# A four-layer kernel (two S4 convolutions, two sliding attentions): the written orders of all five plans laid anew

## The chip, the cores and the metric

The kernel runs on one core of one Trainium2 chip. The core has engines with instruction streams of their own: TensorE (PE, with its weight loads as PEld), VectorE (DVE), ScalarE (ACT), GpSimd (POOL) and SyncE (SP), whose queue issues most DMAs (SPq). Each engine takes its instructions strictly in the order in which they were written; an instruction that waits for another engine holds up everything behind it on its own.

The metric is the time of one execution on the device, in microseconds (us), as the median over runs. A profiled execution has a time of its own beside the span that its trace covers.

## The reference, cut to what matters

The input is one sequence `x` of 2048 positions by 512 channels, in bf16. Four layers follow, each with a residual and a layer norm ahead: S4, attention, S4, attention.

```
def _A_ref(u, ...):            # S4: a kernel K of 2048 taps per channel, then a causal convolution by FFT
    A = A_re + 1j*A_im; dB = exp(log_dt) * (B_re + 1j*B_im); Cc = C_re + 1j*C_im
    P = exp(dt*A * l)          # l = 0..2047, 128 modes per channel
    K = einsum("dn,dnl,dn->dl", Cc, P, dB).real
    y = irfft(rfft(pad(u)) * rfft(pad(K)))[:L] + u * Dskip
def _B_ref(x, wqkv, wo):       # 32 heads of 16; each position sees itself and 7 others, 2 apart
    logits = einsum(q, k at pos - 2*w) * scale, -1e9 where pos - 2*w < 0
    o = einsum(softmax(logits), v at pos - 2*w);  return o @ wo
x = x + _A_ref(layernorm(x)); x = x + _B_ref(layernorm(x))
x = x + _A_ref(layernorm(x)); x = x + _B_ref(layernorm(x))
```

The same parameters serve both S4 layers, so the taps K are built once.

## The kernel before

The sequence lies in SBUF as `X` (128 partitions, 16 columns `j` of 512 channels each) and stays there through all four layers. The program is five plans, run one after another, with no barrier between them:

- Plan 0, `prepare` (L501): the parameters, a ladder of powers of the modes by repeated squaring (`sq`, `lad`, `l`: the square on ACT at L623, the rest on DVE at L631 and L635), multiplier tables from it (`MUA`, `MUB`, `MPA`, `MPB`, one half each at L595 on ACT or L607 on DVE), the first tables of powers `Ttab` (L407 to L428), and the first layer norm, whose sums come from PE as `gram` and `rows` (L678, L682). The first products of the raw parameters (`t`, `quad`, L512) wait for their loads.
- Plan 1, `kernel_and_first_conv` (L724): for eight half-blocks of channels the tables of powers (DVE L412 to L428 and L476, with sums on PE L451 and evictions on ACT L456), the contraction with C and B on PE (L489), the spectra of taps and input (first Fourier step on PE, L863, evicted to `Z` on ACT, L868; transposes by DMA, L877, or on PE; a second step), the product `pa` on DVE (L953), the inverse (`vp`, `VT`) and the output `ps_y` (L997, L1000), evicted to `X` at L1004. The spectrum of the taps goes to DRAM as `kt_scratch`.
- Plan 2, `b_layer` (L1313): transposes of X or U to U (by DMA L1368, or PE L1362 with an ACT copy L1365), q and k (`ps_qk` L1483, evicted to `qT` and `kT` at L1488), a shifted copy of kT (by DMA or by ACT, L1499), products q times k on DVE (`prod` L1556, 2.2 us each), sums of them on PE (`Lp` L1567), softmax pieces (`L`, `LT`, `sm`, a mask by POOL at L1643, the scaling of the logits at L1636), v (`ps_v` L1511, evicted to `VX` at L1522), products with v on DVE (`prod` L1732), sums on PE (`po` L1748, L1753), evictions `ot` on ACT (L1766), transposes of them by DMA (`oT<-ot`, L1771), and the output projection (`ps_o` L1832) added into X. The adding has several ways: a DVE add straight from PSUM (L1804), an ACT eviction (L1810) with a DVE add (L1813) or with an accumulating DMA issued by POOL (L1816), or an identity matmul on PE (L1829) that adds X in PSUM, with an ACT eviction (L1934 to L1936). Then the layer norm for the next plan (`U`, on ACT L1946 or DVE L196).
- Plan 3, `a_layer` (L1160): the convolution again with the taps' spectrum loaded as `Kt` (sixteen loads on SP, L1298): first Fourier step `ps_s` (L1183) evicted to `Z` (L1187), transposes `zt<-Z` by DMA (L1198) or PE, second step `xp` (L1222 to L1225) evicted to `xc` (L1229), products `pa` (L1239 to L1245), inverse `vp` (L1259, L1263) evicted to `VT` (L1266), outputs `ps_y` (L1285) evicted to X (L1290).
- Plan 4: `b_layer` again, with the output stores on SP (L1970) in place of a layer norm.

No scheduler sets an order while the kernel is built. Each plan first records all its operations with a number each, and `Plan.run` then emits them in the order of a list of numbers written out by hand, one string for each plan (`ORDERS`, L215). Where an operation can be done in several ways (`either`, `moved`, `halved`), each way has numbers of its own, and the way whose numbers stand in the list is the one taken. So the lists set both the order on every engine and the engine of each operation that has a choice. Buffers are reused from small pools (in plans 1 and 3 four PSUM slots `psA`), and a write waits until the slot's last reader is done. The loads of parameters and of the input are issued before plan 0 and are in no list.

Some operations by number, as the prediction's steps and the diff need them:

- Plan 0: 25, 24, 19 are the raw products C_im by B_re, C_re by B_im and C_re by B_re; 26 adds the first two; 14 is the first `quad`; 271, 272, 261 table multiplies; 216 the use of `gram` (L684).
- Plan 1: 330 a first Fourier step on PE, 299 and 300 the sum L452 and its eviction, 301 the table multiply L427 behind it; 429 the product of block 1, part 0, 370 its input's eviction; 237 a store to `k_scratch`; 774 the last `ps_y`, 776 and 775 its eviction on DVE and on ACT.
- Plan 2: 507, 513, 511 products with v; 522 the scaling of the logits L1636.
- Plan 3: 342 and 343 the last eviction of `Z` on ACT and on DVE; 88 the first product; 283 the eviction of `VT` of block 2, part 1, whole on DVE; 408, 411 outputs.
- Plan 4: 417, 500, 497 the transposes L1771; 796, 816, 759 output projections; 508 a sum `po`; 799 an output projection with the identity matmul; 442, 487, 489 products.

Line numbers in the text are those of the profile (where a helper records an operation, the line is the one that emits the instruction).

Of the kernel before, what the change touches and what calls it, by code (L numbers as in the profile page):

```python
# [198 lines left out]
def load_params(nc, pp, prm):  # L199
# [16 lines left out]
    "1 187 185 2 3 7 8 5 9 10 11 12 19 25 24 189 195 14 26 13 256 20 30 27 31 21 34 23 35 45 42 49 38 55 47 48 201 43 "  # L216
    "57 56 39 203 59 61 67 197 199 60 258 69 76 75 68 259 71 260 72 263 83 81 73 87 264 215 84 93 267 95 213 268 88 "
    "85 193 96 191 105 207 100 118 106 205 116 119 120 124 99 209 211 107 128 132 111 134 130 271 135 131 110 280 216 "
    "281 142 218 261 140 146 283 143 219 144 147 108 262 217 284 265 154 266 220 158 152 156 285 125 272 221 155 278 "
    "168 170 222 286 171 159 164 166 269 247 287 229 239 231 233 270 167 273 237 179 178 243 176 288 274 289 275 236 "  # L220
    "276 225 97 223 251 253 227 245 249 241 277 255 279",
    "1 69 70 71 67 68 72 33 2 39 42 40 80 81 82 43 83 0 36 34 37 9 45 86 87 88 77 84 46 49 79 30 89 90 54 199 200 78 "
    "202 203 204 205 47 92 48 206 59 52 53 18 10 19 119 165 20 120 121 122 133 11 134 139 208 209 123 125 126 127 128 "
    "129 210 93 94 136 137 96 97 142 140 143 211 98 27 131 216 28 99 222 57 155 156 62 100 166 159 63 157 144 218 223 "
    "58 158 220 150 219 102 221 224 151 167 162 103 173 163 169 310 311 312 104 105 174 171 313 168 170 152 316 29 "
    "110 317 318 172 64 175 319 153 314 320 284 285 287 288 289 181 117 147 178 182 190 114 148 179 290 183 115 112 "
    "113 193 185 116 184 324 333 194 334 291 325 293 330 322 327 294 118 328 225 226 227 295 331 228 229 188 299 300 "
    "195 248 231 232 233 238 234 340 235 335 237 301 297 390 391 356 303 298 393 394 164 395 308 304 189 305 240 306 "
    "396 250 252 338 357 345 350 339 307 343 397 309 399 400 268 344 416 417 418 242 419 420 422 401 258 270 358 362 "
# [1774 lines left out]
```

## Time and profile before

| | |
|---|---|
| median of 3 runs | 469.04 us (468.52 to 470.63) |
| profiled execution | 469.54 us |
| its span | 467.8 us |
| TensorE clock granted in it, mean | 0.951 |
| plan 0, by DVE | 0 to 54 us |
| plan 1 | 54 to 200 us |
| plan 2 | 200 to 310 us |
| plan 3 | 310 to 359 us |
| plan 4 | 359 to 465 us, then the last store lands |

The 1.7 us between the span and the execution's time lie outside the trace. The page gives, for the whole span, each engine's busy time, its busy tenths in 40 equal slices, and the chain of work that ended last; the answers of the trace give waits, instructions in time, and windows. A busy engine is no proof of a bound; where an engine stands still, the releaser named beside the wait tells what it waited for. DVE's times here are start and duration; the next instruction can start some 0.08 us before the last one's recorded end, so a run of equal instructions goes at a pitch a little under the duration.

### The profile page before, as it was taken

The page shows a single profiled execution, that of the slowest core. Times are in us where ns is not written, and L with a number is a line of the kernel's source. Part 1 is how long each engine was busy: PE and PEld are TensorE (multiplying, and loading weights), DVE is VectorE, ACT ScalarE, POOL GpSimd, SP SyncE. Part 2 cuts the span into 40 slices and gives each one's busy share as a digit, 9 for nine tenths or more (in the row PEclk, how much of TensorE's full clock was granted, in tenths as well). Part 3 has the DMA queues.
Part 4 walks back from the last instruction along what each step waited for, and adds up shares of the span by engine and source line. Part 5 has one row for each costly group of instructions (what it writes and reads, how often), then busy time and mean ns, then how long its engine had stood idle before and what let it go on. Part 6 is the DMA issues. An engine that isn't in the chain of part 4 may idle for free.

```text
span 467.8 us, 12351 instructions
## 1 busy us (share of the span) xinstructions
PE 393.4 (84%) x5219; PEld 241.4 (52%) x5238; DVE 438.6 (94%) x583; ACT 351.7 (75%) x558; POOL 22.4 (5%) x91
## 2 busy tenths in 40 slices
PE   2330777778889999889999979979998999998896
PEld 1230444555656767634466434656775445664353
DVE  6999999999999998689999998999996999999996
ACT  7999959886789889556786448999996668863351
POOL 1000000000000002200100000000000001000130
PEclk9655799989999999999999989999999999999999
DMA  8981065137399483630021431469937100222594
GB/s 225 204 315 56 3 115 137 25 91 149 84 182 223 92 186 101 137 78 19 36 79 56 91 67 21 111 223 175 188 54 131 39 6 14 79 79 45 57 168 126
DMA packets 111979, 49.88 MB, mean 107 GB/s; under 512 B 88859, under 2 KB 105132, under 8 KB 111668
## 3 DMA queue, kind: packets, MB, share of 16 engines
q1 hardware_dynamic: 110212, 48.10, 46.4%
q0 software_dynamic: 1424, 0.74, 1.4%
q8 instruction: 41, 0.67, 0.6%
q10 hardware_dynamic: 288, 0.26, 0.2%
q14 instruction: 14, 0.11, 0.1%
HBM read 15.88 MB, written 8.13 MB: 51 GB/s over the span
## 4 chain that ended last, share of the span: by engine, by line
PE 43%; DVE 36%; ACT 7%; issue 5%; SPq 5%; DMA 3%; DVEq 0%; ACTq 0%
PE ps_qk L1483 8%; PE po L1748 7%; PE ps_v L1511 5%; DVE Ttab L476 5%; DVE prod L1556 5%; PE ps_o L1832 4%; DVE Y2tab L476 4%; DVE Ttab L413 3%; DVE Ttab L420 3%; PE Lp L1567 3%; SPq L672 3%; DVE Ttab L412 2%; DVE prod L1732 2%; DVE Ttab L428 2%; DVE pa L953 2%
## 5 line engine op out<-in xcount | busy, mean ns | idle before, releaser
L1732 DVE TENSOR_TENSOR prod<-VX,L 128x512 bf16<-128x512 bf16 (+2 forms) x72 | 75.3, 1099 | 1.4 <-PE po L1748 0.7
L1556 DVE TENSOR_TENSOR prod<-qT,kT 128x4096 bf16<-128x4096 bf16 (+1 forms) x40 | 72.3, 1855 | 2.1 <-ACT qT L1488 1.6
L1483 PE MATMUL ps_qk<-U,wqk 128*128 128x512 bf16 x256 | 58.0, 379 | 1.3 <-ACT U L1365 1.1
L1748 PE MATMUL po<-prod,sb_ident 128*128 128x512 bf16 x216 | 51.8, 379 | 3.4 <-DVE prod L1732 3.0
L1483 PEld LDWEIGHTS <-wqk 128*128 128x128 bf16 x256 | 24.2, 98 | 33.2 <-issue 6.2
L1748 PEld LDWEIGHTS <-sb_ident 128*128 128x128 bf16 x224 | 21.6, 98 | 28.9 <-DVE prod L1732 2.7
L451 PE MATMUL ps_sum<-Ttab,sb_ident 128*128 128x512 bf16 x36 | 14.6, 406 | 21.2 <-DVE Ttab L412 21.1
L1832 PE MATMUL ps_o<-wo_t,oT 128*128 128x512 bf16 x122 | 31.8, 383 | 0.3
L868 ACT CAST Z<-ps_s 128x1024 bf16<-128x1024 f32 (+1 forms) x32 | 29.2, 978 | 3.6 <-PE ps_s L863 3.6
L1511 PE MATMUL ps_v<-wv,U 128*128 128x256 bf16 x256 | 31.2, 272 | 0.7 <-ACT qT L1488 0.2
L1522 ACT ACTIVATE VX<-ps_v,rs 128x256 bf16<-128x256 f32 x64 | 26.4, 474 | 6.9 <-PE ps_v L1511 6.4
L1511 PEld LDWEIGHTS <-U 128*128 128x128 bf16 x256 | 24.7, 97 | 7.7 <-issue 2.1
L476 DVE TENSOR_TENSOR Ttab<-Ttab,MPA 128x2048 bf16<-128x2048 bf16 (+2 forms) x20 | 28.1, 1431 | 0.0
L1766 ACT CAST ot<-po 128x1024 bf16<-128x1024 f32 x14 | 14.0, 1012 | 18.0 <-PE po L1748 18.0
L476 DVE TENSOR_TENSOR Y2tab<-Ttab,MPB 128x6144 bf16<-128x6144 bf16 (+1 forms) x13 | 27.2, 2120 | 0.0
L489 PE MATMUL psk<-Ttab 128*32 128x64 bf16 x1024 | 21.2, 201 | 5.7 <-DVE Ttab L476 4.3
L1488 ACT CAST kT<-ps_qk 128x512 bf16<-128x512 f32 x32 | 18.7, 585 | 9.0 <-PE ps_qk L1483 9.0
L167 DVE BATCH_NORM_STATS2 ln_st_a<-X 128x6 f32<-128x512 bf16 x40 | 24.6, 678 | 0.5 <-ACT X L1936 0.3
L489 PEld LDWEIGHTS <-Ttab 128*32 128x32 bf16 x1024 | 19.1, 99 | 10.1 <-issue 9.2
L1488 ACT CAST qT<-ps_qk 128x512 bf16<-128x512 f32 x32 | 18.5, 585 | 7.0 <-PE ps_qk L1483 6.8
L456 ACT CAST Ttab<-ps_sum 128x1024 bf16<-128x1024 f32 (+1 forms) x22 | 18.2, 867 | 7.1 <-PE ps_sum L452 6.9
L1567 PE MATMUL Lp<-prod,sb_bones 128*32 128x512 bf16 x256 | 20.2, 395 | 3.0 <-DVE prod L1556 3.0
(242 smaller groups left out, 991.1 us busy)
## 6 DMA issues: line engine op xcount, KB each, us to landing
kt_scratch<-sp_k SPq DMA_DIRECT2D x16, 256.0 KB, 3.3
Kt<-kt_scratch SPq DMA_DIRECT2D x16, 256.0 KB, 5.3
X<-in_A_u_dram SPq DMA_DIRECT2D x8, 256.0 KB, 5.3
X<-in_A_u_dram SPq DMA_DIRECT2D x4, 512.0 KB, 5.5
out_dram<-X SPq DMA_DIRECT2D x16, 128.0 KB, 2.1
k_scratch<-KTq SPq DMA_DIRECT2D x7, 256.0 KB, 2.7
KT<-k_scratch SPq DMA_DIRECT2D x7, 256.0 KB, 3.1
VX<-VX SPq DMA_DIRECT2D x4, 448.0 KB, 3.7
```

The source lines that it names most:

```text
L476: nc.vector.tensor_tensor(d, src.to_broadcast([128, c, n, 2 * EYB]), mm, ALU.mult)
L489: nc.tensor.matmul(o.rearrange("e (s i) -> e s i", s=2), xs, T[:, 1:3, h, m // 2, :, t], start=(m == 0), stop=False, skip_group_check=True)
L868: nc.scalar.copy(box["Z", kind, dc][:, 0:n // 8, :, jq * 32:(jq + 1) * 32].rearrange("p g r k -> p r g k"), box.pop(("s1", kind, dc, jq))[ ...
L1483: nc.tensor.matmul(ps[:], wqk[:, ct, f0:f0 + 128], XT[:, ct // 2, 4 * s:4 * s + 4, ct % 2, :], start=(ct == 0), stop=(ct == 3))
L1488: copy((qT, kT)[which][fp][:, f2, o:o + 512], box.pop(("qk", which, fp, f2, s))[:])
L1511: nc.tensor.matmul(ps[:, jj].rearrange("p t h d -> p (t h d)"), XT[:, ct // 2, j + jj, ct % 2, :], wv[:, ct, fp * 256:(fp + 1) * 256], sta ...
L1522: nc.scalar.activation(out, ps, ACT.Identity, scale=r)
L1556: nc.vector.tensor_tensor(pr[:], windows(q, 0, 2), windows(kT[fp][:, a:a + n2, col(w):col(w) + 1024], -DIL * 128, 2), ALU.mult)
L1567: nc.tensor.matmul(Lp[r0:r0 + 32, w // 4, :], bones[:, w % 4 + k, :], pr[:, k, f2 - a, hb * 512:(hb + 1) * 512], start=(n == 1 and k == 0) ...
L1732: nc.vector.tensor_tensor(p2[:].rearrange("p w j t d h -> p w (j t) d h"), windows(v, -DIL * 256, taps), l.to_broadcast([128, taps, nj * 2 ...
L1748: nc.tensor.matmul(po[:, c:c + 512], ident[:], p2[:, t, k + j:k + j + 2].rearrange("p j t d h -> p (j t d h)"), start=first, stop=stop)
L1832: nc.tensor.matmul(ps, oT[:, ft // 2, o:o + 128], wo_t[:, ft, :], start=(ft == 0 and not res), stop=(ft == 3))
```

## The change

All five strings of `ORDERS` are replaced; nothing else differs, line for line. No operation is new. The order of most neighbours changes a little on every engine, and in 30 or so places another way of an operation is taken:

- Plan 0: one half of a multiplier goes from DVE to ACT, one normalisation from ACT to DVE; 19 goes behind 26, 14, 13 and 20; 272 and 261 ahead of 216.
- Plan 1: the last X eviction goes from DVE (776) to ACT (775); one VT eviction is split between DVE and ACT, two swap their split. 330 goes behind 299; 429 five places ahead; on SP the store 237 goes ahead of two transposes of u, 340 and 335.
- Plan 2: one shifted copy of kT goes from DMA to ACT; a small copy (`rs`, L1464) from DVE to ACT; output 11 takes the DVE add and no longer an ACT eviction with a DVE add; output 15 the DVE add in place of the identity matmul with an ACT eviction, output 9 the other way round; of the normalisations one more net goes to ACT. 522 goes ahead of 511.
- Plan 3: Z evictions of block 2 (part 8) and block 3 (part 12) go to DVE, of block 2 (part 12) to ACT; VT of (0,2) goes from a split to ACT, of (2,1) from ACT to DVE; X evictions 1 and 3 of block 3 go to DVE, 2 to ACT. The sixteen Kt loads stand in another order, with thirteen ahead of the first transpose in place of twelve; the transpose of part (2,1) is last on SP.
- Plan 4: one shifted copy of kT goes from ACT to DMA; outputs 12 and 9 take an ACT eviction with a DVE add, 13 the plain DVE add; 2 an ACT eviction with a DVE add in place of the accumulating DMA; 7 the reverse; 6 the identity matmul in place of the accumulating DMA. 417 goes behind 500 and 497.

The head of plan 0, the end of plan 1 and the parts of the others that the list above names, as a diff:

```diff
 ORDERS = [
-    "1 187 185 2 3 7 8 5 9 10 11 12 19 25 24 189 195 14 26 13 256 20 30 27 31 21 34 23 35 45 42 49 38 55 47 48 201 43 "
...
-    "85 193 96 191 105 207 100 118 106 205 116 119 120 124 99 209 211 107 128 132 111 134 130 271 135 131 110 280 216 "
-    "281 142 218 261 140 146 283 143 219 144 147 108 262 217 284 265 154 266 220 158 152 156 285 125 272 221 155 278 "
...
-    "195 248 231 232 233 238 234 340 235 335 237 301 297 390 391 356 303 298 393 394 164 395 308 304 189 305 240 306 "
...
-    "754 727 761 762 771 773 768 770 777 778 774 776",
...
-    "440 506 447 501 488 484 482 486 489 766 507 767 764 511 513 491 423 508 765 492 770 503 521 522 523 771 524 768 "
...
-    "222 224 1 0 121 122 13 6 5 20 27 34 21 29 39 41 44 128 135 3 4 35 45 140 130 136 54 229 145 7 2 9 14 11 142 55 "
...
-    "386 213 396 361 271 363 272 398 399 387 374 389 376 274 400 402 275 276 217 417 414 411 278 418 412 313 314 310 "
-    "416 311 408 410",
...
-    "410 463 464 479 413 349 477 465 412 414 478 480 466 350 467 474 353 418 420 415 432 433 417 483 487 488 491 493 "
-    "485 492 486 515 489 494 434 490 441 498 516 501 503 517 507 495 502 504 518 519 520 500 796 497 508 797 521 505 "
...
-    "911 895 896 926 897 925 853 854 866",
+    "1 3 7 8 9 185 191 25 24 189 26 2 5 10 11 12 14 13 20 19 21 30 23 34 27 31 42 35 45 195 55 47 48 49 56 43 38 57 "
...
+    "267 96 197 105 118 100 116 122 123 99 120 97 106 268 215 119 132 128 271 107 134 135 130 211 213 209 280 108 272 "
+    "131 261 216 218 110 281 142 219 283 140 143 147 217 146 111 144 262 152 284 159 158 154 220 285 221 156 265 155 "
...
+    "641 718 719 711 712 666 721 688 728 739 729 722 714 668 663 664 724 725 731 741 748 758 759 750 742 733 753 761 "
+    "754 762 734 777 768 778 771 770 773 774 775 578 727 689",
...
+    "486 439 488 440 501 484 489 764 768 765 447 507 491 492 508 521 513 522 769 423 511 523 766 767 770 771 514 503 "
...
+    "222 224 20 121 27 34 122 29 21 7 39 41 35 15 6 1 0 44 10 9 128 135 140 3 45 54 130 136 48 142 55 145 147 229 5 "
...
+    "396 271 363 272 373 386 387 389 398 399 374 376 400 402 274 275 276 217 417 414 283 415 419 408 313 410 314 310 "
...
+    "462 349 353 477 464 427 352 465 413 466 467 474 350 412 414 487 415 478 480 493 418 432 488 494 491 420 433 492 "
+    "483 434 489 490 441 501 485 498 495 486 500 502 503 504 507 515 816 516 517 518 519 520 796 497 505 817 521 417 "
...
+    "909 910 865 895 911 926 896 897 925",
 ]
```

## The prediction

> **What bounds the kernel now.** First the page's busy shares and slices.
>
> ```profile
> PE 393.4 (84%) x5219; PEld 241.4 (52%) x5238; DVE 438.6 (94%) x583; ACT 351.7 (75%) x558; POOL 22.4 (5%) x91
> ...
> PE   2330777778889999889999979979998999998896
> PEld 1230444555656767634466434656775445664353
> DVE  6999999999999998689999998999996999999996
> ...
> PE 43%; DVE 36%; ACT 7%; issue 5%; SPq 5%; DMA 3%; DVEq 0%; ACTq 0%
> ```
>
> A slice is 11.7 us. DVE (94%) stands at 9 up to slice 15 (about 180 us), with PE at 7 or 8 over most of that: plans 0 and 1 are bound by DVE. From slice 17 (200 us) PE is at 9 almost everywhere: plans 2, 3 and 4 are bound by PE, and DVE's idle time there costs only where PE starves. Engine totals bar little of a reorder; a relaid order can win only idle time on the bounding engine, and lose what it adds there. So the second view is what DVE waited for, whole span.
>
> ```profile
> DVE X L1290 <- PE ps_y L1285: 4.5, 2, 3.3
> DVE dtw L530 <- ACT dtb L528: 3.2, 1, 3.2
> DVE pa L953 <- PE vp L977: 2.3, 1, 2.3
> DVE X L1004 <- PE ps_y L1000: 2.3, 2, 1.3
> DVE prod L1556 <- ACT qT L1488: 1.6, 2, 1.3
> ...
> DVE own L684 <- PE gram L682: 0.6, 1, 0.6
> ...
> DVE L L1636 <- POOL L L1643: 0.5, 1, 0.5
> DVE t L512 <- DMA raw_B_im<-in_A_B_im_dram: 0.4, 1, 0.4
> DVE Ttab L427 <- ACT Ttab L456: 0.4, 1, 0.4
> ```
>
> The columns are total, times and longest. Three waits stand before 180 us and after the first load: raw_B_im (7.05), gram (28.02), Ttab (107.91), 1.4 us in all. That is all that plans 0 and 1 can win. Third, the joint between plans 1 and 2 and the end, in time.
>
> ```profile
> 199.06 0.68 DVE L1004 CAST X<-ps_y 128x512 bf16<-128x512 f32 x1
> 199.77 3.06 DVE L167 BATCH_NORM_STATS2 ln_st_a<-X 128x6 f32<-128x512 bf16 x5
> 199.79 0.62 PE L1362 MATMUL pt_x<-sb_ident,X 128*128 128x128 bf16 x8 [1.37 <-DVE X L1004]
> ```
> ```profile
> 433.81 1.04 ACT ot L1766 x2
> 434.85 5.04 DMA oT<-ot
> 439.89 0.05 issue
> 439.94 0.61 PE ps_o L1832 x2
> 440.54 1.73 PE po L1748 x8
> ```
>
> PE stood idle 1.37 us for one X eviction that sat on DVE behind two statistics. At the end the chain goes through one transposing DMA; from 439.94 PE is busy to 463.99 almost without a gap, so whatever PE must do there is paid.
>
> **The change, part by part.** The sum is made against the profiled execution: 469.54 us, its span 467.8 and 1.7 around it. It lies 0.5 above the median, 469.04.
>
> *Plan 0, start.* The product of C_re and B_re (0.68, pitch 0.6) loses fourth place on DVE and now follows the wait for raw_B_im at 7.05 that it used to precede. One DVE product more stands behind the wait: quad, PE's ptq and the ladder start 0.45 to 0.6 later. I take +0.5. But at 28.02 DVE waited 0.61 for gram, which hangs on the transposes of X and not on the ladder, and the new order puts two table multiplies (L705/L706, 0.6 and 0.44) ahead of it. The wait is filled: -0.6. Behind the L686 that follows, the sum of DVE's work is the same. One multiplier half (0.29) leaves DVE and one normalisation (0.42) comes: +0.1, pitch against pitch. Plan 0: 0.0, between -0.6 (loads seen earlier) and +0.6 (gram late as well).
>
> *Plan 1.* At 107.91 DVE waited 0.35 for ACT's Ttab eviction (106.86 to 107.87), fed by PE L452 at 105.80. One PE half-group (L863, 0.45) now stands later, so L452 can start when DVE's table is there (105.22): -0.35, the whole wait; bounds -0.35 and 0. On DVE the rest are swaps of neighbours. The tightest is the L953 product of dc 1, c 0, five places earlier at 136.45; its input's ACT eviction ended 137.06 in second place, now stands first of its pair, 0.9 earlier at 136.15. Cover 0.3; gone, it costs its lateness. On SP the store at 108.80 goes ahead of two transposes (each 1.3) and moves them 4 to 5 us; PE used them at 115.72 and 116.98, and now has them first at 116.98 and last near 120. A late half-eviction of VT goes from ACT to DVE, and the last X eviction from DVE to ACT: 0.6 to 0.7 each way, DVE even.
>
> *The joint.* That X eviction (0.68 on DVE, 199.06 to 199.74) now runs on ACT behind its matmul, at 198.45 for 0.58, ending 199.03. ACT stood idle there (0.38 of 2 us busy in 198 to 200). PE's pt_x starts 199.1 in place of 199.79: -0.7. Everything from U to the first prod (209.80) follows it. Bounds -0.7 and 0, the latter if a U transpose on SP (L1368) holds the first prod instead.
>
> *Plan 2.* The kT shift of one group becomes an ACT copy (0.86 by the row of the same line's second form, 387.20) where it was a DMA; ACT is 13 to 16 of 20 us busy in 220 to 260, so I cost it nothing; without that cover, 0.86. The L scaling (L1636, 280.67) moves ahead of one 2.2 us prod, to 278.46, where the mask of POOL it needs is ready only at 279.36: DVE stops 0.9. PE works on earlier products until about 283 and then follows DVE: between 0 and 1.05, I take +0.25, near the low end since PE is 2.00 of 2 busy. In the tail (297.3 to 309.2) the chain goes over ACT's evictions and normalisations: one more normalisation net (0.70 pitch) less one output eviction (0.48): +0.2, between -0.2 and +0.7. Out 9 takes the identity matmul (0.22) that out 15 gives up: 0.
>
> *Plan 3.* DVE gains 2 evictions net (+2.3 us), ACT loses 1.9. DVE's room: it waited 3.28 at 358.15 and 1.22 at 354.17; the VT half-group at L1266 moved whole to DVE ends 354.15, before PE's finals at 354.63 need it. Cover 0.5. One early eviction moved to DVE (L1187, 1.22) ends near 326.7, where ACT's ended 329.17, so the last channel block's transposes start 2.5 earlier, and the DMA zt<-Z of 334.72 (3.98, on the chain) lands before PE wants it: PE waited 0.15. The sixteen Kt loads change order, 13 and not 12 of them before the transposes: the last lands by 313 (0.43 issue, 5.3 landing), first used 318.65. I take -0.15; bounds -0.8 (ACT had been the feeder) and +0.6 (DVE late).
>
> *Plan 4.* DVE has hardly any idle time from 381 to 445, and the same work stands ahead of the chain's prod at 429.55: 0. Of the transposes L1771, the one issued at 425.63 goes behind those of 434.85 and 436.18: issued 437.6, landing 5.0, there at 442.6; PE wants it at 443.4 behind two outputs and one po group. Cover 0.8. POOL loses two accumulating DMAs and gains one; out 6 takes the identity matmul instead: PE +0.22 in a stretch with no gap. In the last 10 us one output moves ahead of the last products; PE stays busy and DVE's last add ends level. +0.2, between 0 and +0.7.
>
> Sum: 0.0 - 0.35 - 0.7 + 0.25 + 0.2 - 0.15 + 0.2 = -0.55: 469.0 for a profiled execution like this one. Against the median, 469.04, it gives **468.5**.
>
> A clock row bears on PE's waits.
>
> ```profile
> 268.00:270.00 2.00, 1.01 (x11) 0.69 (x10) 2.00 (x2) 1.37 (x3) 0.00 (x0) 1.00 0.00 0
> 270.00:272.00 2.00, 0.80 (x16) 0.48 (x19) 2.00 (x2) 1.03 (x2) 0.00 (x0) 1.00 0.61 115
> 272.00:274.00 2.00, 1.62 (x24) 0.41 (x12) 1.95 (x2) 0.00 (x0) 0.00 (x0) 0.55 0.95 185
> 274.00:276.00 2.00, 2.00 (x12) 0.63 (x6) 1.94 (x1) 1.01 (x1) 0.00 (x0) 0.60 0.49 93
> ...
> 434.00:436.00 2.00, 0.70 (x3) 0.31 (x4) 2.00 (x2) 1.74 (x2) 0.00 (x0) 1.00 0.00 0
> ```
>
> Columns: window, then busy time of PE, weight load, DVE, ACT, POOL, then granted clock. Four us of PE half idle were followed by four us at 0.55 and 0.60, 1.7 us of full speed lost; the thinner 434 to 436 was not. The Trainium skill (TensorE: Matmul & The Clock Gate, Part 1) says the clock halves after an idle window of some 3.4 us that runs freely, so the same wait may or may not trip it; by it a relaid order could add or drop such a stretch anywhere, and the sum would be +1.15 with one in the tail. The trace agrees in kind: it shows both outcomes for similar idle shares.
>
> **The rivals.** (a) *A half-clock stretch in plan 4's tail.* PE now has a 1.3 us hole at 438.6 while it waits for oT, since DVE's prods run 0.6 to 0.9 earlier there and two outputs that need oT stand before the next po group. If that hole and the 1.3 of 434 to 436 together drop the clock, 1.7 us are paid in full: 468.5 + 1.7 = 470.2, slower; should the third transpose land late as well and hold PE for one po group (1.73), 471.9. For: 272 to 276. Against: 434 to 436 stayed at 1.00. It decides from two us idle in four.
>
> (b) *DVE becomes the bound of plan 3.* +2.3 us on DVE against 4.5 of waiting at its end. If its products run 2 us late at 351.7, where its plan now ends with the whole VT half-group, the cover of 0.5 is gone and PE's finals follow it: +1.5, 470.0, slower. It decides from 0.5 us late. Against: the Z evictions (L1187) that feed the products come 0.3 to 0.5 earlier.
>
> (c) *The feeders gain.* If plan 3 and the tail of plan 2 were held by ACT, whose slices there are 9, its 1.9 us come back (1.75 beyond the 0.15 counted), the L scaling costs nothing (0.25) and the tail stands at its low end (0.4): 468.5 - 2.4 = 466.1. Against: PE was busy 19.84 of 20 us in 320 to 340 and can't go faster.
>
> (d) *Nothing moves:* the joint is held by U's transpose and the Ttab wait returns: 469.4.
>
> **How the numbers follow.** Forecast 0.36, (d) 0.07, (a) 0.18, half of it at its upper end, (b) 0.08, (c) 0.19. The remaining 0.12 go to the bounds at their bad ends together (0.6 + 1.05 + 0.7 + 0.6 + 0.7, less the 1.05 gained at 107.91 and the joint): 469.04 + 2.6 = 471.6. A measurement here tells about 0.5% (2.3 us, 466.7 to 471.4) from no change. Faster is (c) and a low tail of the forecast's own, 0.04: 0.23. Slower is the bad ends and the upper end of (a): 0.21. Same, the rest: 0.56. Range 466.0 (c) to 471.6 (bad ends); the forecast's own is 467.5 to 469.8.
>
> **What would show it.** Plan 0: own (L684) without a wait, quad 0.5 later. No wait at Ttab L427. pt_x within 0.1 of an ACT eviction, DVE's statistics unbroken. L1636 with a wait of 0.9 on POOL. A last X eviction on DVE behind PE with less than 3.28 idle. PE's ps_o one longer in the tail. Wrong: new DVE idle between 30 and 180 us, a granted clock below 0.9 after 380 us, or a plan whose length changes by over 1 us.

## The result and the profile after

The changed kernel takes 473.38 us (median of 4 runs, 472.72 to 473.94) against 469.50 for the kernel before beside it: ratio 1.0074, 95% interval 1.0055 to 1.0093. By the ratio it is 3.5 us slower; the two medians lie 3.9 apart. The profiled execution takes 473.70 with a span of 471.9, 4.1 more than the span of before.

Set against four marks in the two traces, the 4.1 us lie like this. The first mark is the first `pt_x` of plan 2 (L1362), the second the first `ps_s` of plan 3 (L1183), the third the first `pt_x` of plan 4.

| stretch | before | after | difference | predicted |
|---|---|---|---|---|
| plans 0 and 1, with the joint | 199.79 | 200.14 | +0.35 | -1.05 |
| plan 2 | 107.76 | 107.89 | +0.13 | +0.45 |
| plan 3 | 51.43 | 53.70 | +2.27 | -0.15 |
| plan 4 and the last store | 108.82 | 110.17 | +1.35 | +0.2 |

The page of after: busy time, two rows of the slices, and the chain's shares.

```profile
PE 395.5 (84%) x5220; PEld 242.1 (51%) x5239; DVE 439.9 (93%) x583; ACT 351.8 (75%) x558; POOL 21.2 (4%) x90
...
PE   2420777789889989899999899979998999999896
...
DVE  6999999999999997689899999989897999999995
...
PE 39%; DVE 35%; ACT 8%; issue 6%; SPq 5%; DMA 5%; POOL 0%; DVEq 0%; ACTq 0%
```

DVE is busy 1.3 us more in a span that is 4.1 longer, so 2.8 us of waiting were added to it; its row has three new 8s, in slices 19, 26 and 28 counted from 0; the last two (307 to 319 and 330 to 342 us, a slice being 11.8) lie in plan 3. DMA's share of the chain rose from 3% to 5%. What DVE waited for, over the whole span (total, times, longest), with the lines that the prediction did not have:

```profile
DVE X L1290 <- PE ps_y L1285: 2.8, 2, 2.6
...
DVE pa L953 <- ACT sp_k L890: 2.6, 1, 2.6
...
DVE prod L1556 <- DMA wo_t<-in_B_wo_dram: 1.6, 1, 1.6
...
DVE pa L1239 <- PE vp L1263: 1.4, 1, 1.4
...
DVE LT L1585 <- PE Lp L1567: 1.0, 1, 1.0
...
DVE prod L1732 <- DMA VX<-VX: 0.7, 1, 0.7
```

The waits for gram and for Ttab are gone, as predicted. In their place stand one of 2.6 in plan 1 (L953, which turns out below to be for another engine than the one named), one of 1.4 in plan 3 (L1239) and two in plan 4 (L1585, L1732). The joint between plans 1 and 2 answers the prediction closely; instructions in time:

```profile
199.51 0.59 ACT L1004 CAST X<-ps_y 128x512 bf16<-128x512 f32 x1 [1.40 <-PE ps_y L1000]
200.14 0.61 PE L1362 MATMUL pt_x<-sb_ident,X 128*128 128x128 bf16 x8 [0.68 <-ACT X L1004]
```

PE's idle time ahead of `pt_x` went from 1.37 to 0.68. The chain of plan 4:

```profile
401.37 4.74 DMA VX<-VX
...
406.22 2.29 DVE prod L1732
...
438.84 4.96 DMA oT<-ot
...
443.85 1.47 PE ps_o L1832 x6
```

A copy of v (`VX<-VX`) stands on the chain at 401; the end still goes through one transposing DMA, as before. From the mark at the start of plan 4, PE's `ps_o` behind that DMA comes 82.1 us in, against 81.0 before, so some 1.1 of plan 4's 1.35 arose ahead of the tail.

### The profile page after: what moved, and what is told of

It is laid out like the page before. It is cut to its first block, busy times and chain, and to the rows that moved or that the text cites. A ratio compares the mean times of both kernels' runs of the same rounds, so it can differ in the third digit from the quotient of the medians.

```text
span 471.9 us, 12361 instructions
## 1 busy us (share of the span) xinstructions
PE 395.5 (84%) x5220; PEld 242.1 (51%) x5239; DVE 439.9 (93%) x583; ACT 351.8 (75%) x558; POOL 21.2 (4%) x90
## 4 chain that ended last, share of the span: by engine, by line
PE 39%; DVE 35%; ACT 8%; issue 6%; SPq 5%; DMA 5%; POOL 0%; DVEq 0%; ACTq 0%
PE ps_qk L1483 8%; DVE prod L1732 5%; PE po L1748 5%; DVE Ttab L476 5%; DVE prod L1556 4%; PE ps_o L1832 3%; DVE Y2tab L476 3%; DVE Ttab L413 3%; SPq L672 3%; PE Lp L1567 2%; DVE Ttab L420 2%; PE ps_v L1511 2%; DVE Ttab L412 2%; DVE Ttab L428 2%; DVE Ttab L427 2%
## 5 line engine op out<-in xcount | busy, mean ns | idle before, releaser
L1732 DVE TENSOR_TENSOR prod<-VX,L 128x512 bf16<-128x512 bf16 (+2 forms) x72 | 75.2, 1099 | 1.6 <-DMA VX<-VX 0.7
L953 DVE TENSOR_TENSOR pa<-sp_u,sp_k 128x2048 bf16<-128x2048 bf16 x16 | 19.2, 1218 | 5.0 <-ACT sp_k L890 2.6
L1567 PE MATMUL Lp<-prod,sb_bones 128*32 128x512 bf16 x256 | 21.9, 411 | 1.0 <-DVE prod L1556 0.8
```

Of the source, the lines that this page charges most:

```text
L1567: nc.tensor.matmul(Lp[r0:r0 + 32, w // 4, :], bones[:, w % 4 + k, :], pr[:, k, f2 - a, hb * 512:(hb + 1) * 512], start=(n == 1 and k == 0) ...
L1732: nc.vector.tensor_tensor(p2[:].rearrange("p w j t d h -> p w (j t) d h"), windows(v, -DIL * 256, taps), l.to_broadcast([128, taps, nj * 2 ...
```

## The experiments

Unless a kernel changes instructions, it differs only in the five lists. All were timed in rounds against the kernel before; microseconds are the ratio's distance from 1 times the time before. The stretches of a profiled execution come from one execution each, so a single one of them counts for less than a median.

The expectations call the theories by letters. A: each plan's new list costs or gains by itself, and the parts add up. B: what differs is where PE's clock drops to half; such stretches come wherever PE has stood idle, with any list. D: chance in the landing of transfers and in the clock decides, not the order. E: the lists act on each other, one plan's landing the next with less cover.

### One new list at a time

Kernel n3 as the example; n0, n1, n2 and n4 take the new list of their own plan alone.

```diff
 ORDERS = [
...
-    "222 224 1 0 121 122 13 6 5 20 27 34 21 29 39 41 44 128 135 3 4 35 45 140 130 136 54 229 145 7 2 9 14 11 142 55 "
...
+    "222 224 20 121 27 34 122 29 21 7 39 41 35 15 6 1 0 44 10 9 128 135 140 3 45 54 130 136 48 142 55 145 147 229 5 "
...
```

> The kernel before with the new list of plan 0 alone. The prediction's step gives 0.0 with bounds -0.6 and +0.6; theory E would need plan 0's list to shift plan 1 against its own loads: then KT near 165 us lands late here too, and +1.5 to +2 us.

> The kernel before with the new list of plan 1 alone. Theory A (every plan's loss sits in its own list: read off the two traces at the first pt_x of plan 2, the first ps_s of plan 3 and the first pt_x of plan 4, the changed kernel is 0.35, then 0.48, then 2.75 us late, and 4.1 at the end): a DVE wait of 2 to 2.6 us for sp_k at L953 near 181 us, the first pt_x of plan 2 0.3 to 1.0 us later than before (later than in the full change if plan 0's 0.3 is missing), the whole +0.3 to +1.0 us. Theory B (the half-speed stretches of TensorE wander with the moment at which a PE wait falls, whichever list made the wait): the same wait near 181, and a granted clock of 0.5 at 272 to 276 or at 313 to 317 us that comes or goes with plans 2 and 3 unchanged, so anything from -1.5 to +2.8 us in the whole.

> The kernel before with the new list of plan 2 alone. Theory A: first prod of plan 2 one ACT eviction (0.86 us) later after the same pt_x (ten evictions of q and k before it in place of nine), plan 2's end level to +0.5, whole 0 to +0.7 us. Theory B: plan 3 unchanged in its list, but its head (313 to 317 us) may now run at half clock or not; with it +1.7 us more.

> The kernel before with the new list of plan 3 alone. Theory A: plan 3's own list makes the stretch at half clock in its head (313 to 317 us, about 1.8 us lost) and the DVE wait of 1.4 us for vp near 338 us: first pt_x of plan 4 2.0 to 2.5 us later, whole +2.0 to +2.5. Theory B: the waits in plan 3's head are nearly those of before (1.06, 1.59 and 0.30 us of PE standing still before; 0.79, 1.85 and 0.28 after), so with plan 2 as it was the clock stays at 1.00 there; +0.3 to +0.9 us.

> The kernel before with the new list of plan 4 alone. Theory A: +1.0 to +1.6 us, from new DVE waits of 0.9 us at the first LT and of 0.7 us for the copy VX to VX, and the identity matmul. Theory B (plan 4's share is a passing state of the one profiled execution): 0 to +0.5 us.

| new list | ratio, 95% | us | own plan's stretch, before to this |
|---|---|---|---|
| plan 0 | 1.0007, 0.9988 to 1.0025 | +0.3 | with plan 1: 199.79 to 200.52 |
| plan 1 | 0.9976, 0.9955 to 0.9997 | -1.1 | with plan 0: 199.79 to 198.84 |
| plan 2 | 0.9982, 0.9963 to 1.0002 | -0.85 | 107.76 to 106.89 |
| plan 3 | 1.0031, 1.0008 to 1.0053 | +1.5 | 51.43 to 53.12 |
| plan 4 | 1.0019, 0.9994 to 1.0043 | +0.9 | 108.82 to 110.09 |

Plans 3 and 4 carry the loss, plans 1 and 2 alone rather gain, where theory A had +0.3 to +1.0 and 0 to +0.7 for them. But the five add up to +0.7, and the changed kernel costs +3.5.

### The changed kernel again, and pairs

Kernel again is the changed kernel unedited; n12 and n34 take two lists each:

```diff
 ORDERS = [
     the list of plan 0 as before
-    the lists of plans 1 and 2 as before
+    the lists of plans 1 and 2 of the changed kernel
     the lists of plans 3 and 4 as before
 ]
```

> The changed kernel as it is, a second time. Its lists alone on the old kernel gave -1.1 (plan 1), -0.85 (plan 2), +1.45 (plan 3) and +0.9 us (plan 4), together +0.4, yet all five gave +3.9. Theory D (chance in the landing of two loads and in the clock): the load KT<-k_scratch near 165 us lands 3 us after its issue and no longer 5.5, the first prod of plan 2 waits 1 us and not 1.6, plan 3's head may run at full clock; +0.4 to +2 us over the kernel before. Theory E (the lists interact for good): KT again 5 us or more, PE waiting 1.9 us for it at L863, and +3 to +4 us.

> The kernel before with the new lists of plans 1 and 2. Theory D: the two gains add, -2.0 us (-1.5 to -2.5), first pt_x of plan 2 1 us earlier, plan 2 a further 0.9 shorter. Theory E: less than 1 us of gain, with KT landing late near 165 us or the first prod of plan 2 held 1.6 us.

> The kernel before with the new lists of plans 3 and 4. Additive: +2.35 us (+1.8 to +3.0): 1.7 in plan 3 (first ps_s of plan 3 to first pt_x of plan 4, 53.1 us against 51.4) and 1.3 in plan 4 (109.9 to 110.2 against 108.8). If the two lists only lose together with a stretch at half clock in plan 3's head: +3 or more, and the stretch in the clock row at 312 to 318.

Measured: again 1.0080 (1.0049 to 1.0110), +3.75, with stretches of 199.99, 107.28, 53.63 and 110.30; n12 1.0005 (0.9980 to 1.0030), +0.2; n34 1.0068 (1.0049 to 1.0088), +3.2. So plans 3 and 4 together make nearly the whole loss, and what the lists of plans 1 and 2 gain alone (-2.0 in sum) is not there when they stand together. A drift of the reference is a rival to this: n1 to n4 were timed in one session, where the kernel before had a median of 470.40, and n0, again and the pairs in a later one on the same chip, where it had 469.14. The medians of n1, n2 and n12 themselves are 469.12, 469.30 and 469.35. No session holds the single lists and the pairs side by side, so that the lists act on each other (theory E) is not shown. In n34's execution 1.3 of the loss lies in plan 2, whose list is the old one: PE ran at half clock from 202 to 205 us, behind the hole at the joint, and the first product came 1.5 later. That part is chance of the clock (theory B), the stretches of plans 3 and 4 (53.99 and 109.98) are like those of again and n4 (theory A); n3 has 53.12 without a half-clock stretch.

### Where plan 1 loses it

The traces show the place, DVE's wait near 181 us. First DVE in before and in after, then what ended ahead of it in after on ACT and on PE, and last PE ten us earlier:

```profile
180.22 1.22 DVE L953 TENSOR_TENSOR pa<-sp_u,sp_k 128x2048 bf16<-128x2048 bf16 x1 [0.62 <-issue]
```
```profile
181.67 1.23 DVE L953 TENSOR_TENSOR pa<-sp_u,sp_k 128x2048 bf16<-128x2048 bf16 x1 [2.63 <-ACT sp_k L890]
```
```profile
179.72 1.01 ACT L890 CAST sp_k<-xp 128x1024 bf16<-128x1024 f32 x1
```
```profile
181.30 0.27 PE L977 MATMUL vp<-sb_IC,pa 128*128 128x256 bf16 x1
```
```profile
170.62 0.20 PE L863 MATMUL ps_s<-KT,sb_F 128*128 128x64 bf16 x1 [1.87 <-DMA KT<-k_scratch]
```

The view of after puts the wait down to `sp_k`, the taps' spectrum, but ACT had ended that at 180.73, 0.94 before DVE went on. What ended just ahead of it is the eighth `vp` matmul on PE, with which PE is done with one of the two buffers of `pa` that DVE writes to. In all 20 executions, with either list, DVE goes on 0.09 to 0.10 after that matmul. PE was idle for at most 0.11 of the 8 us ahead of DVE's start (0.61 in ktclk). So PE sets the pace here, before the change as after it.

With the old list DVE waits 0.6 to 0.8 at this place, in all 14 executions that have it; with the new one 1.1 to 3.2, in all six. DVE came to it at 179.04 in after and at 179.59 in before, but the old list's executions alone spread from 179.08 to 180.77, so no gain of DVE is shown. What differs is PE. Its idle time from 130 us to DVE's start, with 1.7 more for each 3.4 us at half clock, is 3.3 to 3.8 in the 14 and 3.6 (n1), 4.6 (again), 5.5 (after, ktclk), 5.8 (n12) and 7.0 (mended, below) in the six. Part of it is a wait for loads of taps (`KT<-k_scratch`). SP's queue shows what changed around the first of these loads, before and then after:

```profile
146.94 0.58 SPq L847 DMA_DIRECT2D KT<-k_scratch  x1
147.57 1.24 SPq L877 DMA_TRANSPOSE zt<-Z  x1
148.86 1.06 SPq L945 DMA_DIRECT2D kt_scratch<-sp_k  x2
```
```profile
147.95 0.57 SPq L847 DMA_DIRECT2D KT<-k_scratch  x1
148.57 0.52 SPq L945 DMA_DIRECT2D kt_scratch<-sp_k  x1
149.13 1.76 SPq L929 DMA_DIRECT2D X<-in_A_u_dram  x1
150.94 2.34 SPq L945 DMA_DIRECT2D kt_scratch<-sp_k  x1
```

A transpose of 1.24 us used to stand behind the load; now a 256 KB store and a load of X do. With the old order the two late loads of taps landed 2.8 to 3.4 us after issue. With the new one the first took 3.3 to 5.2 and the second 3.0 to 5.7, and PE stood at L863 for 1.28 (n1), 1.66 (n12), 2.02 (mended) or 1.11 and 1.87 (after). Four of the six executions have 3.4 us at half clock between 140 and 175 us, none of the 14 with the old list: in n12 and mended right behind such a wait, in again and ktclk at 142 us, without one.

Kernel ktclk moves the second load of taps ahead of the stores, and fills a hole at the start of plan 3 (its use is shown further down):

```diff
 # plan 1, in the changed kernel
-    ... 592 593 598 562 575 576 560 669 561 ... 604 599 389 605 571 606 580 623 ... 579 683 681 ...
+    ... 592 593 598 669 562 575 576 560 561 ... 604 599 605 571 606 623 ... 579 683 389 580 681 ...
 # plan 3, the first Fourier step
+                for again in range(4 if (dc, j0) == (0, 4) else 1):
                     for jj in range(nj):
```

> The changed kernel with two edits, each read in its own plan. Plan 1: the load KT<-k_scratch near 165 us goes ahead of a transpose as before, and two stores of sp_k (256 KB each) behind the last transpose of Z. Plan 3: one first-step group (L1183, block 0, column 4) is written four times in place of once, which fills some 1.3 us of the 1.6 to 1.9 us in which PE stands still near 311 us with matmuls that change nothing. If the late load makes the DVE wait for sp_k near 181 us (2.0 and 2.6 us in the two executions of the changed kernel): wait 0.6 to 1.2, first pt_x of plan 2 at 198.6 to 199.2 in place of 200.0. If ACT's and PE's order make it: wait 2 or more still, pt_x at 199.7 to 200.2. If idle PE time in one window trips the half clock: clock 1.00 from 306 to 330 us and plan 3 at 53.0 to 53.2 us in place of 53.6 and 53.7; if the order of plan 3 trips it otherwise: 0.5 for 3.4 us again somewhere in 311 to 320.

Measured 1.0029 (1.0014 to 1.0044), +1.4. The load landed in 3.0 and PE's wait for it was gone, yet a half-clock stretch stood at 142 us, and DVE waited 2.8 at L953; the plan ended at 201.21. So that load alone is not the cause. What is shown: the place, the wait for PE, and that the new list brings longer landings or lost clock ahead of it each time. Which of the moved stores and loads brings them was not separated.

### Plan 3

The waits of n3, which has the new list of this plan alone, on PE and then on DVE:

```profile
335.88 0.39 PE L1222 MATMUL xp<-zt,sb_C 128*128 128x512 bf16 x1 [1.16 <-DMA zt<-Z]
```
```profile
337.90 2.36 DVE L1239 TENSOR_TENSOR pa<-xc,Kt 128x2048 bf16<-128x2048 bf16 x2 [1.38 <-PE vp L1263]
```

DVE waits for PE, which waits for a transpose. All five executions with this list unmended (after, again, n3, n34, ktclk) have PE idle for 1.02 to 1.28 at this place and DVE for 1.25 to 1.81; with the old list DVE waits 0.85 at most for vp at this line. On SP, before and then n3 (a group's time spans its members):

```profile
323.02 4.03 SPq L1198 DMA_TRANSPOSE zt<-Z  x3
327.10 1.52 SPq L1298 DMA_DIRECT2D Kt<-kt_scratch  x3
329.19 7.64 SPq L1198 DMA_TRANSPOSE zt<-Z  x4
```
```profile
326.20 1.54 SPq L1298 DMA_DIRECT2D Kt<-kt_scratch  x3
327.85 10.90 SPq L1198 DMA_TRANSPOSE zt<-Z  x6
```

The transpose of part 3 of block 2 (operation 255) stood ahead of the three Kt loads, and now stands behind them and behind the transpose of a later part. Kernel fix34 is n34 with it put back, and with v of column 2 put back in plan 4; fix34b also gives back to ACT one of the two evictions of `Z` that had gone to DVE:

```diff
 # plan 3
-    ... 186 258 187 14 12 8 ... 103 76 344 255 77 163 ...
+    ... 186 258 187 255 14 12 8 ... 103 76 344 77 163 ...
 # plan 4
-    ... 306 311 320 388 ... 442 392 321 446 448 443 309 302 323 303 384 ...
+    ... 306 311 388 ... 442 392 446 448 443 309 302 320 323 303 321 384 ...
 # fix34b only, plan 3
-    ... 341 161 75 90 343 335 ...
+    ... 341 161 342 75 90 335 ...
```

> The kernel before with the new lists of plans 3 and 4, each with one thing put back. Plan 3: on SP the transpose of Z of block 2, part 3 goes again ahead of the last three of thirteen Kt loads and of the transpose of block 3, part 0. Plan 4: on PE and ACT the v of column 2 goes again behind those of 10 and 14, so that the copy VX to VX can go out 1 us earlier. If these two moves make the new waits: PE's wait of 1.2 us for zt near 336 us and DVE's of 1.4 us for vp behind it go, plan 3 is 52.0 to 52.5 (53.1 with the new list, 51.5 with the old; 0.6 more if its head runs at half clock), DVE's wait of 0.6 for VX goes and plan 4 is 109.4 to 109.7 (110.1 new, 108.6 old). If other moves (the extra evictions on DVE, ACT late with xc) make them: plan 3 stays at 52.9 or more with the wait for vp, plan 4 at 110.0.

> As the kernel with the two moves put back in the new lists of plans 3 and 4 (plan 3 was 53.26 us there with its head at half clock, 54.0 without the moves), and with the last first-step eviction of block 3 (Z, L1187) on ACT again and not on DVE. If DVE's evictions are the rest of plan 3's loss: another 0.5 to 1.1 us less, 52.1 to 52.7 with the head at half clock, 51.5 to 52.1 without. If ACT is the bound once the Z eviction is back on it: no less, 52.6 without and 53.2 with the half clock.

Measured: fix34 1.0020 (0.9998 to 1.0041), +0.9, where n34 had +3.2; fix34b 1.0016 (0.9993 to 1.0039), +0.75. DVE at L1239 in fix34, and its waits at that line from 307 to 361 us in fix34b:

```profile
339.74 2.36 DVE L1239 TENSOR_TENSOR pa<-xc,Kt 128x2048 bf16<-128x2048 bf16 x2 [0.71 <-PE vp L1263]
```
```profile
DVE pa L1239 <- PE vp L1263: 0.5, 1, 0.5
```

The wait fell from 1.38 to 0.71 and to 0.5, and PE's wait for the transpose fell below 0.5. Plan 3 took 53.26 in fix34 (with a half-clock stretch) and 51.73 in fix34b (without one), within the 51.4 to 52.2 of the old list without a stretch; with one the old list has 52.09 and 52.12. From these single pairs the transpose would be about 0.5 of the 1.7 that the new list cost in n3, and the eviction about 0.9. The medians don't show the second: fix34b is 0.2 better than fix34, and each is known to about 1 us. That the two moves of plans 3 and 4 together took most of n34's +3.2 away is measured, though across sessions.

### Plan 4

In after, again, n4 and n34 DVE waits 0.56 to 0.8 for `VX<-VX` (0.71 at 406.22); in after it waits 0.96 for `Lp` at 382.74 (1.0 in the other three), where before it waited 0.50; one more addition into X (0.42) stands ahead of the last product. The v of column 2 (operations 320 and 321) had moved on PE and ACT ahead of those of columns 10 and 14, whose two copies left 1.0 later from the start of the plan. With them put back (fix34, fix34b) the wait for `VX<-VX` is gone and plan 4 takes 109.34 and 109.32, against 109.98 to 110.30 in the four executions that have the wait and 108.4 to 109.0 with the old list (best1, below, has a wait of 0.42 for this copy with the old list). In ktclk, with the new list, the copy landed in 3.3 in place of 4.6 to 4.8, in time, and plan 4 took 108.94. So the late copy, by its place and its landing together, is 0.8 or more of the 1.5; the rest was not taken apart.

### Which engine bounds plans 2 to 4

The prediction said PE. Kernel dblv writes three products of DVE twice, one each in plans 2, 3 and 4; dblp writes some matmuls three times:

```diff
 # dblv, L1239 and L1732
+                for again in range(2 if (dc, c) == (1, 0) else 1):
                     nc.vector.tensor_tensor(pr[:], ...
...
+                    for again in range(2 if (fp, j0, w) == (0, 0, 2) else 1):
                         nc.vector.tensor_tensor(p2[:]...
 # dblp, L1181 and L1482
-                for jj in range(nj):
+                for jj in list(range(nj)) * (3 if (dc, j0) == (3, 4) else 1):
...
-                for ct in cts:
+                for ct in list(cts) * (3 if (which, fp, f2, s) == (0, 1, 1, 0) else 1):
```

> The kernel before with one DVE product written twice in each of the plans 2, 3 and 4 (L1732 of group 0, w = 2, 2.2 us of pitch, in plans 2 and 4; L1239 of block 1, part 0, 1.14 us, in plan 3); the second writing gives the same values. Theory of the prediction (PE bounds plans 2, 3 and 4, DVE has room): plan 3 +0 to +0.4, plans 2 and 4 +0 to +0.8 each, whole +0 to +2. Rival (DVE bounds them, so that each new wait or eviction on it is paid): plan 3 (first ps_s to the next pt_x, 51.5 before) +1.0 to +1.2, plan 4 (from pt_x to the end, 108.6 before) +1.8 to +2.3, plan 2 (107.6 before) +1.5 to +2.3, whole +4.3 to +5.6.

> The kernel before with PE groups written three times in place of once: the first step of block 3 at column 4 (L1183, 0.45 us each, +0.9) in plan 3, and one ps_qk group of q (L1483, 0.86 us each, +1.7) in plans 2 and 4, in the stretches where PE was busy 10 of 10 us. Theory of the prediction (PE is the bound): plan 3 +0.7 to +0.9, plan 4 +1.4 to +1.7, plan 2 +1 to +1.7. Rival (DVE is the bound, PE only runs at its heels): plan 3 0 to +0.4, plans 2 and 4 0 to +0.7 each.

Measured: dblv 1.0095 (1.0063 to 1.0126), +4.5, as the rival had it (+4.3 to +5.6); dblp 1.0077 (1.0047 to 1.0106), +3.6, as the prediction's theory had it (its parts add up to +3.1 to +4.3). By these, some four fifths of the 5.5 us added on DVE and of the 4.4 added on PE are paid. The single executions agree roughly: in plan 4, 2.2 us more on DVE cost 2.3 (111.10 against 108.82) and 1.73 more on PE cost 0.9; in plan 2 they cost 1.3 and 0.6 against before, 2.3 and 1.6 against fix34b, which has the old list and, like them, no half clock near 272 us. In plan 3 at most 0.75 of 1.14 on DVE and 0.35 of 0.9 on PE were paid, both about the spread of the old list (51.4 to 52.2). So neither engine is the one bound: work added on either is paid for the most part. A window of before, in plan 3, had shown PE, DVE and ACT alike at 97% or more (window; sum of the stretch; then PE, weight load, DVE, ACT, POOL):

```profile
320.00:340.00 20.00, 19.84 (x162) 13.27 (x160) 19.53 (x32) 19.55 (x23) 0.00 (x0) 1.00 1.03 190
```

### A version better than both

Kernel best1 is the kernel before with the new list of plan 2 and the last X eviction of plan 1 on ACT. best2 adds the filler of plan 3 shown with ktclk; best3 moves the loads of the output weights (operation 2 of plan 2) back behind 426, near their old place; best4 fills one hole of plan 2 with matmuls whose result is overwritten:

```diff
 # plan 1
-    "754 727 761 762 771 773 768 770 777 778 774 776",
+    "754 727 761 762 771 773 768 770 777 778 774 775",
 # plan 2: the new list; best3 in it
-    ... 379 290 263 2 385 ... 497 426 494 ...
+    ... 379 290 263 385 ... 497 426 2 494 ...
 # best4, ahead of ps_den
+                    for again in range(30 if center and (fp, j0) == (0, 8) else 0):
+                        nc.tensor.matmul(ps[:], ident[:], ident[:], start=True, stop=True)
```

> The kernel before with the new list of plan 2 and, in plan 1, one number only: the last X eviction on ACT (775 for 776). Theory: the joint between plans 1 and 2 is 1.28 us from the last ps_y to pt_x in place of 1.98, always (it was so in every execution with the new list of plan 1), and plan 2 is 0.5 to 0.9 us shorter with its new list (106.6 to 106.9 against 107.4 to 107.9); together -1.2 to -1.6 us. Rival: what the joint gives comes back at the first prod (kT's shifted copy, issued by SP behind the transposes of U, lands late): -0.5 us.

> The same with the first-step group of plan 3 (L1183, block 0, column 4) written four times, which fills PE's hole near 310 us. If idle time in one window trips the half clock: clock 1.00 from 300 to 330 us and plan 3 at 51.4 to 51.6 us always; against the kernel before, in which plan 3's head ran at half clock in half of the executions seen (0.6 us each), another -0.3 on the average: -1.5 to -2.0 us. If the filling itself costs (the Z evictions behind it later): plan 3 at 51.8 to 52.2, and -1.0.

> The kernel with the joint's eviction on ACT, the new list of plan 2 and plan 3's hole filled, and in plan 2 the four loads of wo_t (128 KB each) put back on SP from right behind the shifted copy of kT to their old place, behind a transpose near 260 us. If these loads delay the copy that the first prod waits for (it landed 2.9 and 3.4 us after its issue in four executions with them behind it, 2.2 in three): landing 2.2, first prod 9.9 to 10.0 us after the first pt_x in place of 10.6, and the whole -1.8 to -2.3 us against the kernel before. If the copy's landing varies by itself: 10.6 again, -1.0 to -1.5.

> The same with 30 matmuls of the identity by itself ahead of ps_den (L1673) of group 0, second half, in plan 2 alone, which fill 1.6 of the 2.06 us in which PE waits for ACT there. If idle time in one window trips the half clock: clock 1.00 from 262 to 280 us (0.5 for 3.4 us in 13 of 17 executions seen so far), plan 2 at 106.6 to 106.9 us, whole -2.0 to -2.8 us. If not: the stretch again and no change from the kernel without these matmuls.

Measured: best1 0.9993 (0.9974 to 1.0011); best2 0.9981 (0.9963 to 0.9999); best3 0.9982 (0.9967 to 0.9996); best4 0.9976 (0.9961 to 0.9992), 468.5 us against 469.75. The last beats both kernels by a small margin; between best2, best3 and best4 the measurement can't tell. Each gained less than its theory had it (-1.2 to -1.6, -1.5 to -2.0, -1.8 to -2.3 and -2.0 to -2.8 against -0.3, -0.9, -0.85 and -1.1). The stretch near 272 us, which 12 of the 17 executions before best3 have, was absent in best4, but in best3 too, without the filler there, so this filler's worth is not shown. The step of best3 was to make the first product of plan 2 earlier: it waits for a shifted copy of kT, whose landing differs between executions of the same list. From the view of transfers (issue, size, median us to landing), n2 and after:

```profile
kT<-kT SPq DMA_DIRECT2D x1, 192.0 KB, 2.2
```
```profile
kT<-kT SPq DMA_DIRECT2D x1, 192.0 KB, 3.4
```

The product starts 9.9 us after `pt_x` with the first and 11.1 with the second (the wait of 1.6 that the trace of after puts down to `wo_t`, loads issued just behind the copy). In best3, with the weights' loads out of the way, it was 2.8 and 10.5, so the landing is late without those loads too; the cause stays open.

### The mends together

Kernel mended is the changed kernel with the edits of fix34b, of best3 and both fillers.

> The changed kernel with all that was found put back: wo_t's loads in plan 2, the transpose on SP and the Z eviction of block 3 in plan 3, the v of column 2 in plan 4, and both holes of PE filled; lists 0 and 1 as changed. If these are the causes of its loss (plan 2's first prod 0.6, half clock in plan 3's head 0.6 and in plan 2 0.5, plan 3's list 1.6, VX 0.7): 469.3 to 470.0 where the kernel before has 469.5 (-0.2 to +0.5 us), plan 3 at 51.5 to 51.9, plan 4 at 109.3 to 109.5. If the loss lies elsewhere: +2 us or more remain.

Measured 1.0042 (1.0022 to 1.0063), +2.0, and not the even result that was expected. Plan 2 takes 106.95, plan 4 108.94, but plan 1 ends at 200.87: DVE waits 3.2 at L953, and a half-clock stretch stands at 171 us. In this execution 1.1 of the loss lies in plans 0 and 1 and 1.0 in plan 3 (52.44, with the filler), where PE still waits 0.62 for a transpose and DVE 1.86 for an eviction of ACT. So the mends take 1.5 to 1.8 off the changed kernel's +3.5 to +3.75, and about half of its loss or more stays without a tested cause.

## Why the prediction was wrong

- *Plan 0, 0.0.* Right: `own` has no wait and comes 0.6 later, as said. n0 shows no change.
- *Ttab, -0.35.* The step that failed is the reading that "plans 0 and 1 are bound by DVE", with three waits that are "all that plans 0 and 1 can win". PE's row has 9s in slices 12 to 15 as well (counted from 0; 140 to 187 us), and DVE's next wait, 0.6 at 180.22, just beyond the bound, is one for PE. A gain of DVE ends there, so the sum should have had 0 here. The wait that was priced was also no property of the order: a wait of 0.28 or more for a Ttab eviction of ACT (L412 or L427, 100 to 110 us) stands in eight of the nine old-list executions that have a half-clock stretch near 100 us, and in none of the five that have none.
- *SP in plan 1.* Only the store at 108.80 was costed. The stores moved behind the late loads of taps were not looked at; there PE lost 2 us more than before (5.5 against 3.45), DVE's wait grew from 0.6 to 2.6, and the mark came 0.35 late, not 1.05 early. With the joint's 0.7 gained as forecast, the rest of plans 0 and 1 was 1.05 slower, where -0.35 was forecast.
- *The joint, -0.7.* Right: `pt_x` starts 1.28 to 1.29 after the last `ps_y` in all ten executions with the eviction on ACT, and 1.98 to 1.99 in all ten others.
- *Plan 2, +0.45.* Measured +0.1 in after, and n2 alone -0.85. The wait of 0.9 at L1636 was 0.12: POOL's mask ended at 280.39 and L1636 started at 280.42. In the ten executions with this list it is 0 to 0.47.
- *Plan 3, -0.15.* The step that failed: "the last channel block's transposes start 2.5 earlier, and the DMA zt<-Z ... lands before PE wants it". It followed only the transposes of the last block. Operation 255, one of the block before, was moved behind Kt loads and another transpose, so PE waited 1.16 for it and DVE 1.38 for PE. Rival (b) had DVE's products late in plan 3 at a price of 1.5, with a chance of 0.08. That the price is near is luck: it put the lateness at 351.7, by 2.3 us more work on DVE, and it came at 336 to 339, by a late feeder. What the added evictions cost is open.
- *Plan 4, DVE "the same work ahead: 0".* The work was the same, its inputs were not: v of column 2 ahead on PE and ACT made two copies late, which cost 0.8 or more.
- *"Plans 2, 3 and 4 are bound by PE."* This is the reading under the last two. It was half of the truth: dblp shows PE to be paid for the most part, dblv DVE as much. With DVE at 9 in nearly every slice as well, a full PE was no proof of one bound. The row from 320 to 340 us, from which the prediction took PE's 19.84 of 20 us, has DVE at 19.53 and ACT at 19.55.
- *The clock.* Rival (a) did not occur: no stretch at half clock between 380 us and the end of PE's work. One came at the start of plan 3, which no rival priced.
- *The range.* It took +0.6 and +0.7 as the worst of plans 3 and 4, and they came at +2.3 and +1.35. Two slips of its own arithmetic change nothing: rival (d), with 1.05 back on 468.5, is 469.55 and not 469.4, and the low end of the range, 466.0, stands for the 466.1 of (c).

The sum of single lists (+0.7) against the whole (+3.5) is not explained. The drift of the reference between the sessions may hold a part of it. The traces show another: n1 and n12 each gain at the joint, but the wait in plan 1 grew from 1.1 (n1) to 2.4 (n12) and 2.6 (after), and half-clock stretches come on top. Whether the lists act on each other was not settled.

## What to carry to other kernels

When an order is relaid, follow each moved DMA to the wait that needs it, past every store and load that now stands around it; engine totals and the first long waits don't show these. Where two engines both stand at 9 tenths, double some work on each before calling one of them the bound. Where the engine that a wait is put down to had long been done, look for what ended just ahead of the start; it can be the reader that gives a buffer back. A gain on an engine counts only up to the next place where that engine waits anyway, so look one wait beyond the stretch that the change touches.

## What was unexpected of the hardware

Half-clock stretches follow a grid. From 40 us to the end of PE's work each lasts 3.413 us, or twice that (6.83 in n0, again and fix34), and within one execution the distances between their starts are multiples of 3.413 (in after 272.69 to 313.65, twelve of them; in n0 101.22 to 271.89, fifty). The windows at the start of plan 3, after first (window; then sum of the stretch, busy time of PE, weight load, DVE, ACT and POOL; granted clock; share and GB/s of DMA), then before and ktclk:

```profile
310.00:312.00 2.00, 0.18 (x3) 0.18 (x4) 2.00 (x4) 2.00 (x3) 0.00 (x0) 1.00 0.97 332
312.00:314.00 2.00, 1.72 (x28) 1.59 (x26) 1.67 (x3) 2.00 (x4) 0.00 (x0) 0.91 0.94 358
314.00:316.00 2.00, 2.00 (x21) 2.00 (x20) 1.74 (x2) 1.47 (x3) 0.00 (x0) 0.50 0.41 126
```
```profile
310.00:312.00 2.00, 0.83 (x12) 0.71 (x12) 2.00 (x2) 2.00 (x3) 0.00 (x0) 1.00 0.66 245
...
314.00:316.00 2.00, 1.99 (x30) 1.59 (x28) 1.68 (x4) 1.82 (x3) 0.00 (x0) 1.00 0.58 109
```
```profile
310.00:312.00 2.00, 1.49 (x28) 1.32 (x26) 2.00 (x4) 2.00 (x4) 0.00 (x0) 1.00 1.01 357
...
314.00:316.00 2.00, 2.00 (x38) 1.92 (x35) 1.65 (x3) 1.79 (x3) 0.00 (x0) 1.00 0.30 64
```

Cut into windows of this grid, the 20 executions show what goes ahead of a stretch (from 60 us on, windows at full clock, PE's idle time as the profile has it). All 21 windows with 2.01 us or more of PE idle were followed by half clock, none of those with less than 1.66 was, and of the 35 between the two 16 were. At this place before had 1.63 idle and kept its clock, after had 1.87 and lost it. The clock was lost here in six of 15 executions without the filler and in none of five with it. That count is small, but with the filler no window from 302 to 316 us had more than 0.92 idle. The Trainium skill (TensorE: Matmul & The Clock Gate, Part 1) has a free-running window of 4096 cycles, 3413 ns, and the trace agrees with the length; its table has the clock drop after an idle window, where here windows that were half to three fifths idle were enough.

The joint has the same risk. Where the X eviction sat on DVE, PE's two holes there came to 2.17 us (1.37 and 0.80), and in two of ten executions (n34, fix34) half clock followed and the first product of plan 2 came 1.5 later. With the eviction on ACT the holes are 0.67 and at most 0.8, together less than any window that was followed by half clock here, and it did not happen in ten executions. Two in ten against none in ten is no proof by itself, so what this adds to the 0.7 of moving the eviction is not measured.
